# Absolute values on ScalarE, small copies set free, and a new order, in a fused mLSTM and ELU feed-forward kernel

## The chip, the cores and the metric

The kernel runs on one core of a Trainium2 chip. The core has a matrix engine (TensorE, PE in the profile), three engines for elementwise work (VectorE or DVE, ScalarE or ACT, GpSimd or POOL) and SyncE (SP), which here only issues DMAs. Each engine takes its instructions in order, and they wait for one another through semaphores. The metric is the device time of one execution in microseconds (us).

## The reference

Two stages stand one behind the other. The first is an mLSTM recurrence over 768 positions for 4 batches and 8 heads of width 40:

```
m_new  = max(f_gate[t] + m, i_gate[t])
f_stab = exp(f_gate[t] + m - m_new);  i_stab = exp(i_gate[t] - m_new)
C = f_stab * C + i_stab * outer(v[t], k[t])
n = f_stab * n + i_stab * k[t]
denom = max(abs(n . q[t]), 1)
y[t]  = sigmoid(o_gate[t]) * (C q[t]) / denom
```

The second is a feed-forward network on the 3072 x 320 result, with 2048 hidden columns: `elu(x @ w_in) @ w_out`. All of it is float32.

## The kernel before

**Tiles.** The recurrence is computed in chunks of 128 positions: 6 chunks times 4 batches are 24 tiles, n = 4 c + b. For a chunk, `gate_chunk(c)` works on the gates of all 32 heads at once: a copy of the running maximum `m0` into the first column of `m` (L427), a scan for the maxima (L428), the decays (L433, L434) and the copy of the last maximum back to `m0` (L435), all on VectorE. For a tile, `attention(n)` makes the products k.q (L555), scales the values by the input gates and appends the gates as a 41st column for the denominators (`va`, L563 and L564), builds the decay weights by a scan (L595, on rows that for the first two chunks are spread by small matmuls, L581), multiplies (L609), and sums the outputs in PSUM (L631, from chunk 1 on L623 too). The state C is carried by L644 and the lines behind it. Then come the denominators (L673, L676, L679), the scaling and the result (L683, L687), its transposition by TensorE (L704) and a split into a high and a low part, `xh` and `xl` (L707, L710).

**Weights.** 18 pieces of `w_in` and `w_out`, called c0 to c17, are loaded as float64 words and turned to high and low float32 parts by `conversion(i)`: two operations on ScalarE (L324, L329), three on VectorE (L333, L338, L343), an addition on GpSimd (L348), and the split by ScalarE and, as a rule, VectorE (L354, L358). c0, c1, c2 belong to the first layer for the first four hidden blocks; c3 and c4 to the second layer for hidden blocks 0, 1 and 2, 3; c5 and c6 (with the second half of c2) to the first layer of hidden blocks 4 to 7; c7 and c8 to the second layer of 4, 5 and 6, 7; c9 to c17 to the rest. Pieces of `w_out` have 640 columns, those of `w_in` 512. Three `wide` buffers hold loaded pieces.

**Feed-forward.** Tiles go through the network in blocks of 2, 3, 3, 3, 3, 3, 3, 2 and 2. A step is one hidden block of 128 for one block of tiles: eight products of layer 1 (L746) into a PSUM tile `h` of which there are two, the ELU (L754, L757, L759), its high and low part (L762, L764), and three products for each tile in layer 2 (L773). The first three blocks of tiles are taken through hidden blocks 0 to 7 first, then through 8 to 15 one after the other. The PSUM buffers `h` are also those of the spread matmuls L581.

**What sets the order.** Every operation is registered by `op` with the engines that may take it, with an estimated time for each, and with what it reads and writes. `Plan.run` then makes a list schedule in estimated time: whenever an engine is free it starts the ready operation of the lowest rank that finds its buffers, on the engine that would end it first, and so each engine's queue is fixed when the program is built. An operation with `"port"` is kept off VectorE while an operation on GpSimd, or another such one, runs in the plan. The string `FIRST` ranks the first tiles (t) and conversions (c). The ranks of the others follow from how many steps ahead of their first use they are wanted: LEAD and SPACE for tiles, LEAD_C for conversions. FFN steps rank behind all that they need.

Of the kernel before, what the change touches and what calls it, by code (L numbers as in the profile page):

```python
# [14 lines left out]
AF = mybir.ActivationFunctionType  # L15
ALU = mybir.AluOpType
# [4 lines left out]
P = 128  # L21
# [162 lines left out]
def tile_mlstm_then_elu_ffn(  # L184
# [11 lines left out]
    nc = tc.nc  # L196
# [3 lines left out]
    H, S = 2 * HH, NC * L  # L200
# [12 lines left out]
    TMAX = max(BLOCKS)  # L213
    WMAX = max(512, W2N * DM)

    FIRST = "t0c0c1c4t1c2c6c5c8t2c3c7c9"

    LEAD, SPACE, LEAD_C = 4, 3, 2

    R2 = 64 + D  # L220
    ROWS = [slice(64 * two, 64 * two + D) for two in range(2)]
# [9 lines left out]
    def copy(e, o, i):  # L231
        nc.scalar.copy(o, i) if e == "ACT" else eng[e].tensor_copy(o, i)
# [28 lines left out]
    def T(name, i, *shape, dt=F32, part=""):  # L261

        if (name, i, part) not in tiles:
            tiles[name, i, part] = pools[name].tile(list(shape), dt, name=name + part)
        return tiles[name, i, part]
# [148 lines left out]
    def gate_chunk(c):  # L414
        def f():
            return T("gates", c, BH, L, part="f")

        def i():
            return T("gates", c, BH, L, part="i")

        def m():
            return T("gates", c, BH, L + 1, part="m")

        KF, KI, KM, FI = ("gates", c, "f"), ("gates", c, "i"), ("gates", c, "m"), ("first", 0)

        def top(e):
            nc.vector.tensor_copy(m()[:, 0:1], m0)  # L427
            nc.vector.tensor_tensor_scan(m()[:, 1:], f(), i(), m0, op0=ALU.add, op1=ALU.max)  # L428

        op({"port": 1, "DVE": 0.6}, top, (KF, KI, ("m0", 0)), (KM,))  # L430

        def log_decay(e):
            nc.vector.tensor_add(f(), f(), m()[:, 0:L])  # L433
            nc.vector.tensor_sub(f(), f(), m()[:, 1:])  # L434
            nc.vector.tensor_copy(m0, m()[:, L : L + 1])  # L435

        op({"port": 1, "DVE": 0.66}, log_decay, (KM,), (KF, ("m0", 0)))
        op({"port": 1, "POOL": 0.4, "DVE": 0.27}, lambda e: eng[e].tensor_sub(i(), i(), m()[:, 1:]), (KM,), (KI,))
        op({"ACT": 0.3}, lambda e: nc.scalar.activation(f(), f(), AF.Exp), (), (KF,))
        op({"ACT": 0.3}, lambda e: nc.scalar.activation(i(), i(), AF.Exp), (), (KI,))  # L440

        def starts(e):

            nc.vector.tensor_copy(first[:, 0:1], f()[:, 0:1])
            nc.vector.memset(f()[:, 0:1], 0.0)

        def parts(e):
            starts(e)
            rest = [f()] + [pools["rest"].tile([BH, L], F32, name=f"rest{j}") for j in range(2)]
            for j in range(3):  # L450
                part = fgs[j * BH : (j + 1) * BH, c * L : (c + 1) * L]
                nc.vector.tensor_copy(part, rest[j])
                if j < 2:
                    nc.vector.tensor_sub(rest[j + 1], rest[j], part)

        if c < SPREAD_BY_PE:
            op({"port": 1, "DVE": 1.5}, parts, (KF,), (FI, KF, ("fgs", c)))
        else:
            op({"port": 1, "DVE": 0.2}, starts, (KF,), (FI, KF))
            op({"SP": 0.06}, lambda e: nc.sync.dma_start(f_d[c], f()), (KF,), (("f_d", c),),  # L460
               nbytes=BH * L * 4)

        def turned():
            return T("ps_a", ("iT", c), P, BH)

        KT = ("ps_a", ("iT", c))
        op({"PE": 0.35}, lambda e: nc.tensor.transpose(turned(), i(), ident[:BH, :BH]),
           (KI, ("ident", 0)), (KT,))
        op({"DVE": 0.19, "ACT": 0.25}, lambda e: copy(e, iT[:, c, :], turned()),
           (KT,), (("iT", c),))  # L470
        if c > 0:

            op({"port": 1, "DVE": 0.42},
               lambda e: nc.vector.tensor_tensor_scan(
                   i(), f(), first, 0.0, op0=ALU.mult, op1=ALU.add),
               (KF, FI), (KI,))
            op({"SP": 0.06}, lambda e: nc.sync.dma_start(b_d[c], i()), (KI,), (("b_d", c),),
               nbytes=BH * L * 4)
# [34 lines left out]
    def attention(n):  # L513
# [11 lines left out]
        def v3():  # L525
            t3 = T("vko", n, P, 3, H, D)
            return [t3[:, j] for j in range(3)]

        def va():
            return T("va", n, P, H, E)  # L530
# [8 lines left out]
        def dec():  # L539
            return T("dec", n, R2, HH, 1)  # L540

        def den(part=""):
            return T("den", n, P, H, 1, part=part)

        def ps(which, *shape):
            return T("ps_a", (n, which), *shape)
# [12 lines left out]

        op({"PE": 1.25}, products, KQ + (("w", n, "room"),), tuple(("ps_a", (n, two)) for two in range(2)))  # L560

        def values(e):
            eng[e].tensor_mul(va()[:, :, 0:D], v3()[0], ib.to_broadcast([P, H, D]))  # L563
            eng[e].tensor_copy(va()[:, :, D:E], ib)  # L564

        op({"port": 1, "POOL": 0.95, "DVE": 0.6}, values, (KV, ("iT", c)), (("va", n),))

        for fn, kw in ((AF.Exp, dict(scale=-1.0)), (AF.Ln, dict(bias=1.0)), (AF.Exp, dict(scale=-1.0))):
            op(act(H * D),
# [46 lines left out]
        def outputs(e):  # L616
# [19 lines left out]

        KY, KU = ("ps_a", (n, "y")), ("ps_a", (n, "u"))
        op({"PE": 1.6 if c else 0.9}, outputs,
           (("w", n, 0), ("w", n, 1), ("va", n)) + (KB + (("C", b),) if c else ()), (KY, ("given", n)))
        if c < NC - 1:  # L640

            def update(e):
                for h in range(H):
                    nc.tensor.matmul(  # L644
                        ps("u", P, HH, E)[ROWS[h % 2], h // 2, :], v3()[1][:, h, :], va()[:, h, :],
                        start=True, stop=True, skip_group_check=True,
                    )

            op({"PE": 0.5}, update, (KK, ("va", n), ("given", n)), (KU,))
            if c > 0:  # L650

                def shrink(e):
                    for two, rows in enumerate(ROWS):
                        cv = C[b][rows, :, two, :]
                        eng[e].tensor_mul(cv, cv, dec()[rows].to_broadcast([D, HH, E]))  # L655

                op({"port": 1, "POOL": 1.06, "DVE": 0.6}, shrink, (("dec", n),), (("C", b),))

            def gather(e):
                for two, rows in enumerate(ROWS):  # L660
                    cv = C[b][rows, :, two, :]
                    u = ps("u", P, HH, E)[rows]
                    if c == 0:
                        copy(e, cv, u)
                    else:
                        nc.vector.tensor_add(cv, cv, u)

            op({"ACT": 0.58, "DVE": 0.5} if c == 0 else {"DVE": 0.64}, gather, (KU,), (("C", b),))


        def denominators(e):
            y = ps("y", P, H, E)
            nc.vector.tensor_scalar(  # L673
                den("neg"), y[:, :, D:E], -1.0, 1.0, op0=ALU.mult, op1=ALU.max
            )
            nc.vector.scalar_tensor_tensor(  # L676
                out=den(), in0=y[:, :, D:E], scalar=1.0, in1=den("neg"), op0=ALU.max, op1=ALU.max
            )
            nc.vector.reciprocal(den(), den())  # L679

        op({"DVE": 0.5}, denominators, (KY,), (("den", n),))
        op(two_in(H * D),
           lambda e: eng[e].tensor_mul(v3()[2], v3()[2], den().to_broadcast([P, H, D])),  # L683
           (("den", n),), (KS,))
# [218 lines left out]
```

## Time and profile before

| | before |
|---|---|
| device time, median of 3 runs | 495.1 us (493.95 to 495.77) |
| the profiled execution's own time | 494.69 us |
| its span, first to last instruction | 492.6 us |
| mean granted TensorE clock | 0.991 of full speed |
| TensorE matmuls busy | 456.1 us |
| VectorE busy | 362.2 us |
| ScalarE busy | 288.4 us |
| GpSimd busy | 117.6 us |

All times inside the trace count from the start of the span. The shares of busy time are averages over a start, in which the weights are converted and the first tiles made, and a long stage of feed-forward steps; they have to be read by stretch.

### The profile page before, as it was taken

How to read it: one execution, taken by the hardware profiler on the slowest of the kernel's cores; microseconds unless marked ns; L12 is line 12 of the kernel's file. 1: busy time of each engine (PE TensorE's matmuls, PEld its weight loads, DVE VectorE, ACT ScalarE, POOL GpSimd, SP SyncE). 2: the span in 40 equal slices, each digit the busy share in tenths (PEclk: the TensorE clock that was granted, in tenths of full speed). 3: DMA queues.
4: the chain of work that ended last, by engine and by line, in shares of the span. 5: the costliest groups of instructions: out<-in, count | busy, mean ns of one | idle time of the engine just before them, and what ended most of it. 6: DMA issues, size and time to landing. Idle time of an engine off the chain costs nothing.

```text
span 492.6 us, 12520 instructions
## 1 busy us (share of the span) xinstructions
PE 456.1 (93%) x5006; PEld 432.6 (88%) x5006; DVE 362.2 (74%) x752; ACT 288.4 (59%) x681; POOL 117.6 (24%) x151
## 2 busy tenths in 40 slices
PE   2535889999999999999999999999999999999997
PEld 2334878999999999999989999999999999999996
DVE  8989898998787987965896478873678365546543
ACT  3555945779876564646456464475447544654664
POOL 2444484244231253121220101430012031000000
PEclk9999979999999999999999999999999999999999
DMA  7665544433325353421441034540333030100000
GB/s 266 176 208 166 167 136 138 134 110 127 106 82 154 100 164 110 154 84 42 133 145 43 28 110 127 153 124 1 111 111 109 1 97 1 43 1 1 28 1 27
DMA packets 39001, 49.51 MB, mean 101 GB/s; under 512 B 3072, under 2 KB 31648, under 8 KB 38944
## 3 DMA queue, kind: packets, MB, share of 16 engines
q1 hardware_dynamic: 38944, 48.72, 31.9%
q8 instruction: 39, 0.64, 0.5%
q14 instruction: 18, 0.15, 0.1%
HBM read 43.32 MB, written 5.39 MB: 99 GB/s over the span
## 4 chain that ended last, share of the span: by engine, by line
PE 86%; DVE 11%; ACT 2%; issue 1%; DVEq 0%; ACTq 0%
PE h L746 36%; PE acc L773 34%; PE ps_a L555 5%; PE ps_a L631 3%; PE ps_a L623 3%; DVE w L595 2%; PE ps_a L644 1%; PE ps_a L704 1%; DVE narrow L343 1%; DVE w L358 1%; DVE narrow L333 1%; DVE e L759 1%; DVE narrow L338 1%; PE h L581 1%; DVE w L609 1%
## 5 line engine op out<-in xcount | busy, mean ns | idle before, releaser
L746 PE MATMUL h<-xh,w 128*128 128x384 f32 (+1 forms) x720 | 179.6, 325 | 3.6 <-DVE w L595 2.2
L773 PE MATMUL acc<-w,gh 128*128 128x320 f32 x768 | 175.4, 315 | 1.5 <-DVE w L358 1.5
L773 PEld LDWEIGHTS acc<-w,gh 128*128 128x128 f32 x768 | 128.3, 189 | 3.9 <-DVE w L358 1.7
L746 PEld LDWEIGHTS h<-xh,w 128*128 128x128 f32 x720 | 126.1, 189 | 6.4 <-DVE w L595 2.6
L759 DVE SCALAR_TENSOR_TENSOR e<-e,h 128x384 f32<-128x384 f32 (+1 forms) x144 | 72.7, 505 | 72.6 <-ACT e L757 71.9
L754 ACT ACTIVATE e<-h 128x384 f32<-128x384 f32 (+1 forms) x144 | 65.4, 454 | 101.8 <-PE h L746 96.0
L773 PE MATMUL acc<-w,gl 128*128 128x320 f32 x384 | 119.3, 311 | 0.0
L746 PE MATMUL h<-xl,w 128*128 128x384 f32 (+1 forms) x432 | 113.0, 320 | 0.0
L762 ACT CAST gh<-e 128x384 fp32r<-128x384 f32 (+1 forms) x144 | 67.8, 472 | 34.9 <-DVE e L759 34.8
L764 DVE TENSOR_TENSOR gl<-e,gh 128x384 fp32r<-128x384 f32 (+1 forms) x118 | 64.1, 544 | 27.0 <-ACT gh L762 23.9
L746 PEld LDWEIGHTS h<-xl,w 128*128 128x128 f32 x432 | 77.1, 189 | 0.0
L773 PEld LDWEIGHTS acc<-w,gl 128*128 128x128 f32 x384 | 72.5, 189 | 0.8 <-DVE gl L764 0.6
L757 ACT ACTIVATE e<-e 128x384 f32<-128x384 f32 (+1 forms) x144 | 70.5, 490 | 3.8
L595 DVE TENSOR_TENSOR_SCAN w<-w,ident 128x512 f32<-128x512 f32 x32 | 40.0, 1249 | 5.6 <-DMA w<-f_d 5.4
L764 POOL TENSOR_TENSOR gl<-e,gh 128x384 fp32r<-128x384 f32 (+1 forms) x26 | 25.4, 978 | 63.2 <-ACT gh L762 59.0
L348 POOL TENSOR_TENSOR narrow<-narrow,wide 128x512 int32<-128x512 int32 (+1 forms) x18 | 27.4, 1523 | 41.9 <-DVE narrow L343 24.5
L570 ACT ACTIVATE vko<-vko 128x320 f32<-128x320 f32 x72 | 33.6, 467 | 2.7 <-DMA vko<-in_vko 1.9
L555 PE MATMUL ps_a<-qk 40*128 40x128 f32 x384 | 32.4, 316 | 0.0
L609 DVE TENSOR_TENSOR w<-ps_a,w 128x512 f32<-128x512 f32 x48 | 31.1, 679 | 1.3 <-PE ps_a L555 0.8
L555 PEld LDWEIGHTS ps_a<-qk 40*128 40x128 f32 x384 | 27.4, 216 | 4.4 <-issue 3.7
L655 POOL TENSOR_TENSOR C<-C,dec 40x164 f32<-40x164 f32 x28 | 16.1, 576 | 60.8 <-PE ps_a L623 59.8
L563 POOL TENSOR_TENSOR va<-vko,iT 128x320 f32<-128x320 f32 x15 | 14.1, 938 | 65.6 <-issue 33.4
(87 smaller groups left out, 419.8 us busy)
## 6 DMA issues: line engine op xcount, KB each, us to landing
vko<-in_vko SPq DMA_DIRECT2D x24, 480.0 KB
w<-f_d SPq DMA_DIRECT2D x32, 256.0 KB
qk<-in_qk SPq DMA_DIRECT2D x48, 160.0 KB
wide<-in_w_out SPq DMA_DIRECT2D x8, 640.0 KB
wide<-in_w_in SPq DMA_DIRECT2D x8, 512.0 KB
out<-os SPq DMA_DIRECT2D x24, 160.0 KB
bb<-b_d SPq DMA_DIRECT2D x40, 80.0 KB
sum<-os SPq DMA_DIRECT2D x8, 160.0 KB
```

What stands on the lines that cost most here:

```text
L348: lambda e: nc.gpsimd.tensor_add(narrow(), narrow(), words()[0]),
L555: nc.tensor.matmul(ps(two, P, HH, L)[:, j, :], kt[rows, j, :], qt[rows, j, :], start=True, stop=True,)
L570: lambda e, fn=fn, kw=kw: nc.scalar.activation(v3()[2], v3()[2], fn, **kw), (), (KS,))
L595: nc.vector.tensor_tensor_scan(a, f, ident4.rearrange("p h t -> p (h t)"), 0.0, op0=ALU.mult, op1=ALU.add)
L609: lambda e, half=half: nc.vector.tensor_mul(w(half), ps(half, P, HH, L), w(half)),
L746: nc.tensor.matmul(h(), a[g][:, fs], m, start=(i == 0), stop=(i == len(prods) - 1))
L754: op(act(N), lambda e, h=h, ff=ff: nc.scalar.activation(ff("e"), h(), AF.Relu, scale=-1.0), (KHP,), (KE,))
L757: lambda e, ff=ff: nc.scalar.activation(ff("e"), ff("e"), AF.Exp, scale=-1.0), (), (KE,))
L759: lambda e, h=h, ff=ff: nc.vector.scalar_tensor_tensor(out=ff("e"), in0=ff("e"), scalar=-1.0, in1=h(), op0=ALU.add, op1=ALU.max),
L762: op(act(N), lambda e, ff=ff: nc.scalar.copy(ff("gh", F32R), ff("e")), (KE,), (KG,))
L764: lambda e, ff=ff: eng[e].tensor_sub(ff("gl", F32R), ff("e"), ff("gh", F32R).bitcast(F32)),
L773: nc.tensor.matmul(acc(a), x[:, sl], bw[g][:, j, :], start=(f == f0 and i == 0), stop=(f == f1 - 1 and i == 2),)
```

## The change

The absolute value of the denominators is taken by ScalarE, straight from PSUM, and VectorE only clamps and inverts it in SBUF. The copies into `m`, back to `m0`, and of the gates into the 41st column of `va` become operations of their own that ScalarE may take (for `va` GpSimd too); the keys of `va` are split for that. `FIRST` and LEAD_C are changed, and the whole program is planned anew.

```
-    FIRST = "t0c0c1c4t1c2c6c5c8t2c3c7c9"
-    LEAD, SPACE, LEAD_C = 4, 3, 2
+    FIRST = "t0c0c4t1c8c5c1c2t2c6c3c7c9"
+    LEAD, SPACE, LEAD_C = 4, 3, 0
...
-        def top(e):
-            nc.vector.tensor_copy(m()[:, 0:1], m0)
-            nc.vector.tensor_tensor_scan(m()[:, 1:], f(), i(), m0, op0=ALU.add, op1=ALU.max)
-        op({"port": 1, "DVE": 0.6}, top, (KF, KI, ("m0", 0)), (KM,))
+        op({"ACT": 0.2, "DVE": 0.13}, lambda e: copy(e, m()[:, 0:1], m0), (("m0", 0),), (KM,))
+        op({"port": 1, "DVE": 0.48},
+           lambda e: nc.vector.tensor_tensor_scan(
+               m()[:, 1:], f(), i(), m0, op0=ALU.add, op1=ALU.max),
+           (KF, KI, ("m0", 0)), (KM,))
+        op({"ACT": 0.2, "DVE": 0.13}, lambda e: copy(e, m0, m()[:, L : L + 1]), (KM,), (("m0", 0),))
...
-            nc.vector.tensor_copy(m0, m()[:, L : L + 1])
-        op({"port": 1, "DVE": 0.66}, log_decay, (KM,), (KF, ("m0", 0)))
+        op({"port": 1, "DVE": 0.54}, log_decay, (KM,), (KF,))
...
-        def values(e):
-            eng[e].tensor_mul(va()[:, :, 0:D], v3()[0], ib.to_broadcast([P, H, D]))
-            eng[e].tensor_copy(va()[:, :, D:E], ib)
-        op({"port": 1, "POOL": 0.95, "DVE": 0.6}, values, (KV, ("iT", c)), (("va", n),))
+        op({"port": 1, "POOL": 0.75, "DVE": 0.49},
+           lambda e: eng[e].tensor_mul(va()[:, :, 0:D], v3()[0], ib.to_broadcast([P, H, D])),
+           (KV, ("iT", c)), (("va", n, 0),))
+        op({"port": 1, "ACT": 0.2, "POOL": 0.2, "DVE": 0.17},
+           lambda e: copy(e, va()[:, :, D:E], ib), (("iT", c),), (("va", n, 1),))
...
+        op({"ACT": 0.22},
+           lambda e: nc.scalar.activation(den(), ps("y", P, H, E)[:, :, D:E], AF.Abs),
+           (KY,), (("den", n),))
         def denominators(e):
-            y = ps("y", P, H, E)
-            nc.vector.tensor_scalar(
-                den("neg"), y[:, :, D:E], -1.0, 1.0, op0=ALU.mult, op1=ALU.max
-            )
-            nc.vector.scalar_tensor_tensor(
-                out=den(), in0=y[:, :, D:E], scalar=1.0, in1=den("neg"), op0=ALU.max, op1=ALU.max
-            )
+            nc.vector.tensor_scalar_max(den(), den(), 1.0)
             nc.vector.reciprocal(den(), den())
-        op({"DVE": 0.5}, denominators, (KY,), (("den", n),))
+        op({"port": 1, "DVE": 0.3}, denominators, (), (("den", n),))
```

## Rows read from the trace of the kernel before

**Rows 1.** The page's first part: busy time, share and instructions of each engine.

```profile
PE 456.1 (93%) x5006; PEld 432.6 (88%) x5006; DVE 362.2 (74%) x752; ACT 288.4 (59%) x681; POOL 117.6 (24%) x151
```

**Rows 2.** Stretches of time: length, busy us by engine, granted clock, DMA.

```profile
core 0: us, PE busy (x) PEld busy (x) DVE busy (x) ACT busy (x) POOL busy (x), PEclk, DMA share, GB/s
0.00:47.00 47.00, 18.35 (x327) 15.08 (x327) 42.77 (x86) 24.00 (x50) 19.18 (x29) 1.00 0.65 209
47.00:75.00 28.00, 24.52 (x310) 21.70 (x311) 24.97 (x56) 19.02 (x50) 15.89 (x21) 0.88 0.49 150
75.00:492.60 417.60, 413.23 (x4371) 395.83 (x4370) 294.50 (x611) 245.38 (x582) 82.54 (x103) 1.00 0.28 85
```

**Rows 3.** TensorE's waits: who, for whom, total us, times, longest.

```profile
PE h L581 <- DVE w L595: 15.9, 5, 8.0
PE acc L773 <- DVE w L358: 1.5, 1, 1.5
```

**Rows 4.** Timeline of TensorE: start us, us, line, operation, idle before and releaser.

```profile
41.82 0.85 PE L704 MATMUL ps_a<-ident,xf 128*128 128x128 f32 x3
...
47.05 0.58 PE L746 MATMUL h<-xh,w 128*128 128x256 f32 x1 [1.72 <-DVE w L595]
...
55.05 0.56 PE L773 MATMUL acc<-w,gh 128*128 128x320 f32 x2 [1.50 <-DVE w L358]
...
81.36 0.34 PE L746 MATMUL h<-xh,w 128*128 128x384 f32 x1
```

**Rows 5.** Timeline of VectorE: tile 1's result; ends of c2, c5, c8, c17.

```profile
31.88 0.49 DVE L687 TENSOR_TENSOR xf<-ps_a,vko 128x320 f32<-128x320 f32 x1
...
34.49 2.37 DVE L358 TENSOR_TENSOR w<-narrow,w 64x512 fp32r<-64x512 f32 x2
...
42.46 0.68 DVE L358 TENSOR_TENSOR w<-narrow,w 128x512 fp32r<-128x512 f32 x1
...
48.21 0.82 DVE L358 TENSOR_TENSOR w<-narrow,w 128x640 fp32r<-128x640 f32 x1
...
147.74 0.79 DVE L358 TENSOR_TENSOR w<-narrow,w 128x640 fp32r<-128x640 f32 x1
```

**Rows 6.** Stretches around the low granted clock (columns as in rows 2).

```profile
65.00:70.00 5.00, 3.69 (x30) 3.28 (x32) 4.90 (x9) 2.07 (x7) 4.85 (x6) 0.78 0.48 119
70.00:80.00 10.00, 10.00 (x218) 9.01 (x217) 8.13 (x18) 4.42 (x12) 7.02 (x10) 0.77 0.45 152
```

**Rows 7.** Stretch 0 to 75 us of L673, L564 and L427 alone.

```profile
core 0: us, DVE busy (x), PEclk, DMA share, GB/s
0.00:75.00 75.00, 0.82 (x5) 0.95 0.59 187
...
core 0: us, DVE busy (x) POOL busy (x), PEclk, DMA share, GB/s
0.00:75.00 75.00, 0.17 (x1) 1.52 (x5) 0.95 0.59 187
...
0.00:75.00 75.00, 0.28 (x2) 0.95 0.59 187
```

**Rows 8.** Groups by line and shape: count, busy us, mean ns, idle before.

```profile
L676 DVE SCALAR_TENSOR_TENSOR den<-ps_a,denneg 128x8 f32<-128x8 f32 x24 | 4.0, 166 | 0.8
L679 DVE RECIPROCAL den<-den 128x8 f32<-128x8 f32 x24 | 4.9, 203 | 0.8
L232 ACT COPY iT<-ps_a 128x32 f32<-128x32 f32 x4 | 0.7, 177 | 0.1
L595 DVE TENSOR_TENSOR_SCAN w<-h,ident 128x512 f32<-128x512 f32 x16 | 19.0, 1207 | 0.5 <-PE h L581 0.4
L609 DVE TENSOR_TENSOR w<-ps_a,w 128x512 f32<-128x512 f32 x48 | 31.1, 679 | 1.3 <-PE ps_a L555 0.8 <-ACT wl L232 0.2
```

**Rows 9.** Timeline of GpSimd and VectorE: L333 beside L348, and alone.

```profile
20.09 1.28 POOL L348 TENSOR_TENSOR narrow<-narrow,wide 128x512 int32<-128x512 int32 x1 [3.23 <-ACT vko L570]
20.35 1.38 DVE L333 TENSOR_SCALAR narrow<-narrow 128x640 f32<-128x640 f32 x1
...
48.95 0.48 DVE L333 TENSOR_SCALAR narrow<-narrow 128x640 f32<-128x640 f32 x1
```

**Rows 10.** The chain that ended last, in order of time: last steps of block 0.

```profile
146.57 1.92 PE h L746 x16
...
151.66 1.76 PE acc L773 x12
```

More of the change, by code (lines that the diff above doesn't have):

```diff
@@ L540, in dec, with den @@
             return T("dec", n, R2, HH, 1)
-        def den(part=""):
-            return T("den", n, P, H, 1, part=part)
+        def den():
+            return T("den", n, P, H, 1)
         def ps(which, *shape):
@@ L638, in attention @@
         op({"PE": 1.6 if c else 0.9}, outputs,
-           (("w", n, 0), ("w", n, 1), ("va", n)) + (KB + (("C", b),) if c else ()), (KY, ("given", n)))
+           (("w", n, 0), ("w", n, 1), ("va", n, 0), ("va", n, 1)) + (KB + (("C", b),) if c else ()), (KY, ("given", n)))
         if c < NC - 1:
@@ L647, in update @@
                     )
-            op({"PE": 0.5}, update, (KK, ("va", n), ("given", n)), (KU,))
+            op({"PE": 0.5}, update, (KK, ("va", n, 0), ("va", n, 1), ("given", n)), (KU,))
             if c > 0:
```

## The prediction

> **What bounds the kernel now.** I read the busy times first, then the share of each engine in stretches of time, then TensorE's own waits, then the timeline around the places that these point at. TensorE is busy for 456.1 of 492.6 us, VectorE for 362.2 [rows 1]. The stretches show where the 36.5 us without a matmul lie: 28.65 of them before 47 us, 3.5 between 47 and 75, and 4.4 in all the 417.6 after that [rows 2]. From about 81 us on this is a TensorE kernel, and nothing that VectorE, ScalarE or GpSimd does there can be seen unless it becomes later than TensorE's queue. Up to about 75 us VectorE is the bound: it is busy for 67.7 of 75 us [rows 2]. TensorE's waits say the same: 15.9 us of them are attention's spread matmuls (L581) that wait for a VectorE scan to free the PSUM buffer that they share with the FFN [rows 3]. So one number stands for the whole start: the first product of 384 columns, where the block of three tiles begins, at 81.36 us [rows 4]. Behind it lies a fixed amount of TensorE work; what moves that start moves the end.
>
> Three readings inside the start matter. First, tile 1's result was finished by VectorE at 32.37 us [rows 5], yet its transposition ran at 41.82 [rows 4], since TensorE takes its queue in order and two spreads that waited for scans stood before it. Secondly, the first product of layer 1 ran at 47.05, and layer 2 began at 55.05, released by the last VectorE operation of the w_out conversion c3 [rows 3, 4]. Thirdly, TensorE was busy for only 3.69 of the 5 us from 65 and then ran at a lower granted clock: 0.78 of full speed on average from 65 to 70 us and 0.77 from 70 to 80 [rows 6], with the lower of the two levels (1.2 GHz) in between. At 2.4 GHz this stretch would have cost 0.22 x 5 + 0.23 x 10 = 3.4 us less.
>
> **The change, part by part.** Terms are against the profiled execution's own time, 494.69 us: span 492.6 and 2.09 around it. That execution is 0.4 below the median of the three (495.1) and inside their spread.
>
> (a) Less on VectorE before 75 us. Five tiles run their denominators there [rows 7]. Before, each takes a maximum (0.16), a combined maximum (0.17) and a reciprocal (0.20) [rows 7, 8], 0.53 us; after, one maximum, taken at 0.16 like the nearest one-input row, and the reciprocal: 0.17 less, five times, 0.83. The `va` copy ran once on VectorE in that time (0.17; the other five were on GpSimd already), and the two gate chunks' copies into `m` took 0.28 [rows 7]; the copies back to `m0` (L435) are as many and as small, another 0.28. If all go to ScalarE that is 1.56 us. Nothing of ScalarE's share is on the path: its nearest row, a copy of 128x32 from PSUM, takes 0.18 us [rows 8], and it is idle for 32 of the first 75 us [rows 2]. Without that cover an absolute value would cost its 0.18 plus whatever conversion work queues behind it on ScalarE while it waits for the outputs' matmuls; VectorE's first denominator operation waits at that place today, so the wait moves with it and is not new. Queued behind it on ScalarE are the next conversion's L324, L329 and L354 and the L570 of the next tile, and VectorE waits for those; but VectorE has other work of that kind at hand all through the start. The copy into `m` adds one wait on the path of chunk 0, where VectorE's scan comes right behind it: between 0 (VectorE keeps the copy) and 0.18 for ScalarE's copy less the 0.14 that VectorE saves; taken as 0.
>
> What stands against it: the new maximum reads and writes SBUF, where the old one read PSUM. The trace shows what an SBUF-only operation with a constant can meet: L333 at 128x640 took 1.38 us while GpSimd's addition ran from 20.09 to 21.37, and 0.48 when it ran at 48.95 beside an idle GpSimd [rows 9]; the reciprocal, also in SBUF and with one input, shows no stretch in its mean of 203 ns over all 24 [rows 8], so both ends are possible for a new form. If it stretches, GpSimd being busy for 35.1 of 75 us (47%) [rows 2], a maximum meets one of its operations about every second time and waits for half of it, 0.64: 0.47 x 0.64 x 5 = 1.5 us, which would eat the gain. Bounds: 0 and 1.5. I take 0.7, since the planner now keeps this operation out of GpSimd's planned time but real times differ from planned ones. The Trainium skill, "SBUF — State Buffer", section "Who interferes with whom", has the rule for the second end: VectorE and GpSimd share one pair of ports as an exclusive lock, and a copy or an operation with a constant that uses both ports fully blocks until the other engine's instruction is over. By that rule alone the term would be -1.5 and (a) nil; L333's end, 0.36 us after GpSimd's, agrees with it. (a) = -1.56 + 0.7 = -0.85 us.
>
> (b) The order of the first conversions. Before c3, the same work stands in both orders: tiles 0 to 2 and c0, c1, c2, c4, c5, c6, c8. So the last VectorE operation ahead of layer 2 should end at about the same time, and I take nothing. Within that, tile 1 comes ahead of c1, and c1 and c2, which the first product needs, come behind c8 and c5. Tile 1's product is thus ready earlier (it stood waiting for 9.5 us anyway) and c2 later: c2 ended at 36.86 before [rows 5] and had 10.2 us in hand until 47.05. It was the fourth conversion loaded and is now the sixth; three `wide` buffers hold the loads, so it follows the second and third buffer to come free. Bounds: the two scans (1.21 each) and two products (0.68 each) of tile 3 that ran on VectorE ahead of c3's end although they rank later [rows 8] could fall behind it, -3.8 us; or c2 could become the bound, +3.5 (below).
>
> (c) The pause near 65 us. VectorE with less to do should reach the scan and the FFN step that TensorE waited for some tenths of a us earlier. I expect that the pause becomes short enough for the clock to stay up. TensorE then gets 3.4 us back, but only as much is worth having as VectorE can follow: in the low-clock stretch from 70 to 80 us VectorE stood idle for 1.87 us [rows 6]. So -1.9, with the bounds 0 and -3.4.
>
> (d) Later conversions ranked two steps later (LEAD_C). The last one ended at 148.53 [rows 5], and the two steps of layer 2 that use it began at 151.66 [rows 10]: 3.1 us in hand. Two steps of two tiles are 1.92 + 1.76 = 3.7 us of TensorE [rows 10], so it could lose 0.6 us, and only if the planner let it wait for all of its new rank. Taken as 0.
>
> (e) Past 148 us every removed or moved operation lies beside TensorE work: 0. The gate copies gain a wait between engines per chunk, off the path there.
>
> Sum: -0.85 - 1.9 = -2.75, so 491.9 us.
>
> **Rivals.**
> *A much shorter start.* Tile 3's scans fall behind c3, so layer 2 starts 3.8 us earlier, all of the 1.56 arrives, and the pause vanishes: 494.69 - 3.8 - 1.56 - 1.9 = 487.4. For it: tile 1's transposition need not wait behind spreads, as TensorE reaches them sooner. Against it: the spreads are placed by a planner that fills idle TensorE time with whatever fits, which was what let tile 3 in.
> *The relief is eaten.* The new maximum meets GpSimd as L333 did, and the pause and the low clock stay: 494.7. For it: 47% GpSimd share; against it: the order is planned around that.
> *Slower: c2 becomes the bound.* Place: the first product of layer 1. As a late load c2 could end where the seventh conversion ended before, c8 at 49.03, plus 1.55 for its second half (2.37 against 0.82) [rows 5]: 50.6. The first product is then 3.5 us later than 47.05, layer 2 behind it as well, and the end: 498.2. It decides from the point where c2's last operation ends later than 47 us. For it: two w_out conversions, the longer kind (640 columns against 512), hold two of the three buffers ahead of it. Against it: the sixth load before, c5, was done by 43.14 us [rows 5], inside the time in hand.
>
> **How the numbers follow.** A measurement of this kernel can tell about 0.5%, 2.5 us, from no change: faster ends at 492.6, slower begins at 497.6. Forecast 0.44 (from 489.7 to 494.7, a little more than half of it under 492.6: 0.26 faster, 0.18 same); the shorter start 0.24, all faster; the eaten relief 0.12, all same; c2 late 0.20, all slower. Together 0.50, 0.30 and 0.20. The range reaches from 487 to 498.5: it takes in both bounds of (a), (b) and (c) less the corners where several fall together.
>
> **What would show it.** (a): denominators of two VectorE operations and one of ScalarE, none of VectorE's maxima beyond 0.3 us where GpSimd is idle, VectorE's sum before 75 us smaller. (b): tile 1's transposition before 35 us, c2's last operation after 38 but before 47, layer 2 near 54. (c): granted clock 1.00 from 65 to 80 us, and the first product of 384 columns at about 78.6 instead of 81.36. (d): no TensorE wait between 130 and 155 us. The prediction is wrong if that first 384-column product moves and the end doesn't move with it, or if TensorE gains new pauses behind 81 us.

## The result

The changed kernel takes 490.24 us (median of 7 runs, 490.01 to 491.43) against 495.03 (7 runs, 492.77 to 496.36): ratio 0.991, 95% interval 0.989 to 0.993. It is faster by 0.9%. The profiled execution has an own time of 490.24 and a span of 488.4, 4.2 less than the span of before. The forecast was 491.9.

The page's first part, of after [against rows 1]:

```profile
PE 459.8 (94%) x5006; PEld 434.2 (89%) x5006; DVE 368.7 (75%) x745; ACT 298.3 (61%) x746; POOL 80.4 (16%) x93
```

TensorE was busy for longer than before (459.8 against 456.1) in a shorter span: what fell is its idle time, 488.4 - 459.8 = 28.6 us against 36.5. GpSimd lost a third of its work (80.4 against 117.6), ScalarE gained 9.9 us.

Stretches of after, columns as in [rows 2]; the last three answer to [rows 6]:

```profile
0.00:47.00 47.00, 26.93 (x362) 22.04 (x362) 43.54 (x85) 29.46 (x72) 18.44 (x26) 1.00 0.72 229
47.00:75.00 28.00, 24.89 (x291) 22.49 (x294) 24.50 (x52) 18.35 (x51) 8.97 (x11) 0.82 0.37 105
75.00:488.40 413.40, 407.97 (x4375) 389.71 (x4362) 300.71 (x610) 250.47 (x623) 53.00 (x56) 1.00 0.28 87
...
60.00:65.00 5.00, 4.09 (x25) 3.57 (x26) 4.66 (x8) 2.73 (x10) 3.29 (x4) 0.60 0.42 132
65.00:70.00 5.00, 4.56 (x28) 4.07 (x25) 3.95 (x6) 1.75 (x4) 1.01 (x2) 0.50 0.36 106
70.00:75.00 5.00, 5.00 (x92) 4.65 (x95) 4.21 (x10) 2.49 (x8) 0.91 (x2) 0.88 0.22 63
```

TensorE gets ahead in the first 47 us: 362 products instead of 327, and 20.1 us without one instead of 28.65. From 60 to 75 us the granted clock is low, 0.60, 0.50 and 0.88; before it was low only from 65 us on (0.78 from 65 to 70 and 0.77 from 70 to 80 [rows 6]).

TensorE's waits of after, as in [rows 3]:

```profile
PE h L581 <- DVE w L595: 11.5, 6, 3.2
```

The wait of 8.0 us is gone, the longest is 3.2, and the sum for L581 fell from 15.9 to 11.5. Layer 2's wait of 1.5 us for c3 is gone as well: its first product, at 52.42 below, has no idle time before it. A wait for a later conversion, c7, stands at 66.53.

Timeline of TensorE in after, columns as in [rows 4]:

```profile
27.45 0.90 PE L702 MATMUL ps_a<-ident,xf 128*128 128x128 f32 x3
...
41.41 0.56 PE L744 MATMUL h<-xh,w 128*128 128x256 f32 x1
...
52.42 0.46 PE L771 MATMUL acc<-w,gh 128*128 128x320 f32 x2
...
60.91 0.54 PE L581 MATMUL h<-fgs,sel 96*128 96x128 bf16 x4 [2.04 <-DVE w L595]
...
64.01 2.08 PE L555 MATMUL ps_a<-qk 40*128 40x128 f32 x16
...
66.53 0.90 PE L771 MATMUL acc<-w,gh 128*128 128x320 f32 x2 [0.44 <-DVE w L358]
...
82.61 0.45 PE L744 MATMUL h<-xh,w 128*128 128x384 f32 x1
```

Tile 1's transposition came 14.4 us earlier than in [rows 4], the first product of layer 1 5.6 and layer 2 2.6. Then comes a pause of 2.04 us before 60.91, the lower clock behind it (the 16 products of L555 took 2.08), and the first product of 384 columns 1.25 us later than before.

How can the end come 4.2 us earlier, if that product comes later? A start of one operation says only how far that operation got. I counted all products that had started by a point, each kind at a fixed time taken from its groups at full clock in these traces (0.118 us for 256 columns in layer 1, 0.176 for 384, 0.147 in layer 2, 0.0725 in L555, and so on). The sum is an estimate of the TensorE work done, in us; the last column is the span:

```
by (us)                       47    60    75    85   110   span
before                      11.9  21.2  31.2  41.9  66.5  492.6
after                       15.4  25.1  34.8  43.7  68.8  488.4
order alone (e4)            14.4  21.9  31.2  41.6  66.2  491.9
old denominators (e11)      14.7  24.9  33.3  42.4  66.8  492.0
copies on VectorE (e12)     14.7  24.3  32.3  41.5  66.4  490.8
one pause filled (e9)       15.3  25.1  33.3  42.5  67.5  491.8
pauses filled, 58-67 (e10)  15.3  25.1  35.9  45.0  69.8  488.1
```

After is 3.5 us of work ahead by 47 us and still 2.3 ahead by 110. (With the small products at the distance from one start to the next, 0.068 us in L555, every sum is 3 to 7 us lower, but a row's distance from the row of before changes by at most 0.5.) The first 384-column product is later because more of the attention work and of the two-tile steps ran before it.

### The profile page after: what moved, and what is told of

It is laid out like the page before. It is cut to its first block, busy times and chain, and to the rows that moved or that the text cites. A ratio compares the mean times of both kernels' runs of the same rounds, so it can differ in the third digit from the quotient of the medians.

```text
span 488.4 us, 12469 instructions
## 1 busy us (share of the span) xinstructions
PE 459.8 (94%) x5006; PEld 434.2 (89%) x5006; DVE 368.7 (75%) x745; ACT 298.3 (61%) x746; POOL 80.4 (16%) x93
## 4 chain that ended last, share of the span: by engine, by line
PE 83%; DVE 9%; ACT 3%; DMA 3%; issue 1%; POOL 0%; SPq 0%; DVEq 0%; ACTq 0%
PE h L744 35%; PE acc L771 33%; PE ps_a L555 5%; PE ps_a L631 4%; PE ps_a L623 3%; DVE w L595 2%; PE ps_a L644 1%; PE ps_a L702 1%; DMA bb<-b_d 1%; DVE narrow L343 1%; PE h L581 1%; DMA w<-f_d 1%; DMA wide<-in_w_in 1%; DVE w L358 1%; DVE e L757 1%
## 5 line engine op out<-in xcount | busy, mean ns | idle before, releaser
L744 PE MATMUL h<-xh,w 128*128 128x384 f32 (+1 forms) x720 | 184.7, 329 | 2.9 <-DVE w L595 1.6
L744 PEld LDWEIGHTS h<-xh,w 128*128 128x128 f32 x720 | 128.2, 193 | 6.0 <-DVE e L757 2.2
L762 DVE TENSOR_TENSOR gl<-e,gh 128x384 fp32r<-128x384 f32 (+1 forms) x132 | 70.3, 537 | 31.8 <-ACT gh L760 30.8
L744 PEld LDWEIGHTS h<-xl,w 128*128 128x128 f32 x432 | 78.5, 193 | 0.0
L595 DVE TENSOR_TENSOR_SCAN w<-w,ident 128x512 f32<-128x512 f32 x32 | 38.9, 1217 | 6.7 <-DMA w<-f_d 6.6
L348 POOL TENSOR_TENSOR narrow<-narrow,wide 128x512 int32<-128x512 int32 (+1 forms) x18 | 27.1, 1504 | 52.3 <-DVE narrow L343 21.5
L555 PE MATMUL ps_a<-qk 40*128 40x128 f32 x384 | 34.0, 317 | 0.0
L555 PEld LDWEIGHTS ps_a<-qk 40*128 40x128 f32 x384 | 28.4, 216 | 5.3 <-issue 4.0
L609 DVE TENSOR_TENSOR w<-ps_a,w 128x512 f32<-128x512 f32 x48 | 31.5, 682 | 2.0 <-PE ps_a L555 1.8
L563 POOL TENSOR_TENSOR va<-vko,iT 128x320 f32<-128x320 f32 x18 | 14.4, 808 | 72.3 <-PE ps_a L644 27.4
L631 PE MATMUL ps_a<-va,w 128*32 128x41 f32 x1536 | 21.7, 213 | 0.2
L631 PEld LDWEIGHTS ps_a<-va,w 128*32 128x32 f32 x1536 | 18.5, 118 | 3.2 <-issue 0.6
```

What stands on the lines that cost most here:

```text
L555: nc.tensor.matmul(ps(two, P, HH, L)[:, j, :], kt[rows, j, :], qt[rows, j, :], start=True, stop=True,)
L595: nc.vector.tensor_tensor_scan(a, f, ident4.rearrange("p h t -> p (h t)"), 0.0, op0=ALU.mult, op1=ALU.add)
L609: lambda e, half=half: nc.vector.tensor_mul(w(half), ps(half, P, HH, L), w(half)),
L631: nc.tensor.matmul(y[r, h, :], w()[:, i, r], va()[:, h, :], start=not opened, stop=(i == H - 1), skip_group_check=True,)
L744: nc.tensor.matmul(h(), a[g][:, fs], m, start=(i == 0), stop=(i == len(prods) - 1))
L762: lambda e, ff=ff: eng[e].tensor_sub(ff("gl", F32R), ff("e"), ff("gh", F32R).bitcast(F32)),
```

## Where VectorE's time went

In the kernel before, the last VectorE operation of c3 released layer 2. It ended at 55.00 us before and at 51.23 after, where layer 2 (52.42) no longer waits for it. VectorE's busy time up to there, first before, then after (length, busy and count):

```profile
0.00:55.00 55.00, 24.84 (x370) 20.92 (x370) 49.77 (x98) 30.81 (x66) 22.39 (x32) 1.00 0.65 209
```

```profile
0.00:51.23 51.23, 30.53 (x448) 25.19 (x450) 47.48 (x92) 32.72 (x80) 20.26 (x27) 1.00 0.70 223
```

Of the 3.77 us, 2.29 are less busy time (third pair, 49.77 to 47.48) and 1.48 less idle (5.23 to 3.75). Groups of VectorE's operations in these stretches show which. Before (count, then busy us and mean ns, then idle time ahead and its releaser):

```profile
L358 DVE TENSOR_TENSOR w<-narrow,w 128x640 fp32r<-128x640 f32 x3 | 2.5, 830 | 0.9 <-ACT w L354 0.8
...
L333 DVE TENSOR_SCALAR narrow<-narrow 128x640 f32<-128x640 f32 x3 | 2.4, 784 | 0.0
L358 DVE TENSOR_TENSOR w<-narrow,w 64x512 fp32r<-64x512 f32 x2 | 2.3, 1171 | 0.1
...
L338 DVE TENSOR_SCALAR narrow<-narrow 128x640 int32<-128x640 int32 x3 | 2.0, 666 | 0.1
...
L683 DVE TENSOR_TENSOR vko<-vko,den 128x320 f32<-128x320 f32 x3 | 1.8, 600 | 0.0
...
L673 DVE TENSOR_SCALAR denneg<-ps_a 128x8 f32<-128x8 f32 x3 | 0.5, 161 | 1.0 <-PE ps_a L631 1.0
```

After:

```profile
L358 DVE TENSOR_TENSOR w<-narrow,w 128x640 fp32r<-128x640 f32 x3 | 2.5, 827 | 0.2 <-ACT w L354 0.2
...
L681 DVE TENSOR_TENSOR vko<-vko,den 128x320 f32<-128x320 f32 x3 | 1.5, 497 | 0.0
L338 DVE TENSOR_SCALAR narrow<-narrow 128x640 int32<-128x640 int32 x3 | 1.5, 491 | 0.1
...
L333 DVE TENSOR_SCALAR narrow<-narrow 128x640 f32<-128x640 f32 x3 | 1.4, 476 | 0.0
L358 DVE TENSOR_TENSOR w<-narrow,w 64x512 fp32r<-64x512 f32 x2 | 1.4, 686 | 0.1
...
L676 DVE TENSOR_SCALAR den<-den 128x8 f32<-128x8 f32 x3 | 0.5, 165 | 0.0
```

These are the same operations in the same number (but for the denominators), and four groups lost 2.7 us (2.4 + 2.3 + 2.0 + 1.8 against 1.5 + 1.5 + 1.4 + 1.4); the other shape of L333 gained 0.4. They were stretched beside GpSimd, and are not now. The clearest case is the pair of c2, which took 2.37 us from 34.49 on [rows 5], beside this operation of GpSimd:

```profile
34.69 1.62 POOL L348 TENSOR_TENSOR narrow<-narrow,wide 128x512 int32<-128x512 int32 x1 [1.70 <-DVE narrow L343]
```

In after the pair takes 1.40, at 40.86, with GpSimd idle. The small operations themselves count for less: 1.75 us by their rows left VectorE there (copies into C, which the new plan gave to ScalarE, 0.60; one of the denominators 0.5; the others 0.65), and 1.9 us of other work that ran later before came in (1.3 of FFN steps and a scaling, 0.6 of a product L609 that started at 54.92 before). So nearly all of the 2.29 us is stretching that is gone: 2.7 - 0.4 + 1.75 - 1.9 = 2.15, and rows overlap by some tenths. Of the idle time, 1.0 us was the old denominators' wait for the outputs' products (L673), which now falls to ScalarE's Abs, and 0.6 c3's wait for ScalarE's L354.

## The experiments

**Single parts alone.** e1: the kernel before with the new FIRST. e2: the kernel before with LEAD_C = 0. e4: with both. e3: the changed kernel with the old FIRST and LEAD_C, so the new operations alone.

```diff
# e1
-    FIRST = "t0c0c1c4t1c2c6c5c8t2c3c7c9"
+    FIRST = "t0c0c4t1c8c5c1c2t2c6c3c7c9"
# e2
-    LEAD, SPACE, LEAD_C = 4, 3, 2
+    LEAD, SPACE, LEAD_C = 4, 3, 0
# e4: both of these, on the kernel before
# e3: both of these undone, on the changed kernel
```

> The kernel before with the new string FIRST alone. Theory A (the order of the first conversions makes the gain: tile 1 comes ahead of c1, so TensorE gets tile 1's outputs and transposition some 14 us earlier and begins layer 1 near 41 instead of 47 us): 490.5 to 491.5 us, tile 1's transposition before 30 us. Theory B (the forecast's term: less work for VectorE makes the gain, the order nothing): 494 to 496 us. Theory C (any new plan moves the start by a few us by chance, the parts don't add up): anywhere from 488 to 499, and not with the sign of A.

> The kernel before with LEAD_C = 0 alone. The forecast's step (d) and theory A: no change, 494.5 to 495.5 us, no TensorE wait from 130 to 155 us. The rival to (d), that conversions ranked later reach TensorE late: 495.5 to 497 us with a wait for L358 or L354 in that stretch. Theory C: a shift of 2 us or more in either direction that arises before 85 us.

> The kernel after with the old FIRST and LEAD_C, so the edits of operations alone (absolute value on ScalarE, free small copies). Theory B (relief of VectorE before 75 us): 492 to 493.5 us. Theory A: 494 to 495.5 us, tile 1's transposition still after 38 us. Theory C: off from both by 2 us or more.

> The kernel before with both order edits, FIRST and LEAD_C, and no edit of operations. Theory A: 490.5 to 491.5 us, like FIRST alone. Theory B: 494 to 496 us. Theory C: differs from FIRST alone by 2 us or more though LEAD_C alone does nothing.

Measured against 495.31 (35 runs): e1 493.84, ratio 0.9986 [0.9967, 1.0004]; e2 494.40, 0.9986 [0.9968, 1.0003]; e3 495.11, 1.0000 [0.9983, 1.0018]; e4 493.05, 0.9974 [0.9955, 0.9994]. The operations alone give nothing, the order alone 0.26%, together they give 0.92%. So the two need each other, as far as these kernels tell it: each of them was planned anew, and a plan alone can move more than that (e7 and e11 below). e3's time is the one that theory A expected, but its tile 1 was transposed at 32.05 us, not after 38 (41.82 in before): that this comes early brought nothing there. The times of e1 and e4 lie between what A and B expected. Why the order alone isn't enough, TensorE's waits of e4 show:

```profile
PE h L581 <- DVE w L595: 8.8, 5, 3.5
...
PE h L746 <- DVE e L759: 4.9, 2, 3.4
PE ps_a L631 <- DVE w L609: 3.5, 2, 2.6
```

The long spread wait is gone here too, but TensorE now waits for VectorE elsewhere: for a two-tile FFN step (3.4) and a masked score product (2.6). It is 2.5 us ahead by 47 us and level with before by 75 (the table above). And e4 has a collision of its own. First GpSimd, then VectorE, in its timeline:

```profile
27.12 1.56 POOL L348 TENSOR_TENSOR narrow<-narrow,wide 128x640 int32<-128x640 int32 x1 [3.21 <-DMA gatesf<-in_f_gate]
...
27.53 1.49 DVE L683 TENSOR_TENSOR vko<-vko,den 128x320 f32<-128x320 f32 x1
```

The multiplication vko·den took 1.49 us here and ended 0.34 after GpSimd's addition, as L333 did in [rows 9]. The same operation in before:

```profile
31.36 0.48 DVE L683 TENSOR_TENSOR vko<-vko,den 128x320 f32<-128x320 f32 x1
```

**Parts taken back, planned anew.** e5: the changed kernel with LEAD_C = 2. e7: with the old denominators. e8: with the old copies.

```diff
# e5
-    LEAD, SPACE, LEAD_C = 4, 3, 0
+    LEAD, SPACE, LEAD_C = 4, 3, 2
# e7
-        op({"ACT": 0.22},
-           lambda e: nc.scalar.activation(den(), ps("y", P, H, E)[:, :, D:E], AF.Abs),
-           (KY,), (("den", n),))
...
-            nc.vector.tensor_scalar_max(den(), den(), 1.0)
+            y = ps("y", P, H, E)
+            nc.vector.tensor_scalar(
+                den("neg"), y[:, :, D:E], -1.0, 1.0, op0=ALU.mult, op1=ALU.max
+            )
+            nc.vector.scalar_tensor_tensor(
+                out=den(), in0=y[:, :, D:E], scalar=1.0, in1=den("neg"), op0=ALU.max, op1=ALU.max
+            )
...
-        op({"port": 1, "DVE": 0.3}, denominators, (), (("den", n),))
+        op({"DVE": 0.5}, denominators, (KY,), (("den", n),))
# e8: top(), log_decay() and values() as in the kernel before
```

> The kernel after with LEAD_C back at 2. Theory D (the edits of operations and the new FIRST only work together, LEAD_C is nothing): 489.5 to 491 us. Theory E (a lucky plan that needs all three): 492 to 495 us.

> The kernel after with the denominators as before, three operations on VectorE from PSUM. If the relief of VectorE by the absolute value carries its part of the gain (0.83 us by the forecast's term): 490.8 to 492 us. If the denominators carry nothing: 489.7 to 490.7 us. If only the whole plan works: 492.5 us or more.

> The kernel after with the small copies as before (into m and back to m0 on VectorE inside their neighbours, the gates' column of va on the engine of the product before it). If the forecast's 0.73 us for them holds: 490.8 to 491.5 us. If freeing these copies is what lets TensorE start earlier together with the order: 492.5 us or more. If they carry nothing: 489.7 to 490.7.

Measured against 495.00 (20 runs): e5 490.75, 0.9927 [0.9907, 0.9948]; e7 497.33, 1.0057 [1.0039, 1.0076]; e8 492.89, 0.9961 [0.9943, 0.9979]. LEAD_C is worth nothing that can be measured. Without the Abs the kernel is slower than before. But the planner wrote another order for e7 and e8, so these two mix the operation's price and the plan's. That called for the next pair.

**Parts taken back, the plan kept.** The planner is left with the costs of the changed kernel, so that it writes the same order, and only the function that an operation issues is exchanged. e11: the Abs operation issues nothing, and the VectorE operation issues the old three. e12: the gate copies and the copy into `va` run on VectorE.

```diff
# e11
-           lambda e: nc.scalar.activation(den(), ps("y", P, H, E)[:, :, D:E], AF.Abs),
+           lambda e: None,
...
-            nc.vector.tensor_scalar_max(den(), den(), 1.0)
+            # the two operations of e7
# e12
-        op({"ACT": 0.2, "DVE": 0.13}, lambda e: copy(e, m()[:, 0:1], m0), (("m0", 0),), (KM,))
+        op({"ACT": 0.2, "DVE": 0.13}, lambda e: copy("DVE", m()[:, 0:1], m0), (("m0", 0),), (KM,))
...
-        op({"ACT": 0.2, "DVE": 0.13}, lambda e: copy(e, m0, m()[:, L : L + 1]), (KM,), (("m0", 0),))
+        op({"ACT": 0.2, "DVE": 0.13}, lambda e: copy("DVE", m0, m()[:, L : L + 1]), (KM,), (("m0", 0),))
...
-           lambda e: copy(e, va()[:, :, D:E], ib), (("iT", c),), (("va", n, 1),))
+           lambda e: copy("DVE", va()[:, :, D:E], ib), (("iT", c),), (("va", n, 1),))
```

> The plan of the kernel after, kept to the instruction, but the denominators by the three old VectorE operations at the place of the two new ones, and nothing on ScalarE. If the price of the operations is what counts (0.17 to 0.2 us for each of five tiles): 490.8 to 491.8 us. If the 497.3 of the kernel with the old denominators and a plan of its own came from the operations: 496 us or more. If it came from the plan, as I now think: not above 492.

> The plan of the kernel after, kept to the instruction, but the copies into m, back to m0 and of the gates' column all on VectorE, at their places in the plan. Price of the operations alone (five va copies at 0.17 and three gate copies at 0.14 before 75 us): 490.8 to 491.8 us. If freeing the copies from VectorE is the key: 492.5 us or more.

Measured against 495.32 (20 runs): e11 494.06, 0.9980 [0.9966, 0.9995]; e12 492.54, 0.9947 [0.9930, 0.9964]. So in one and the same order the denominators are worth 494.06 - 490.24 = 3.8 us and the copies 2.3 (3.6 and 1.9 by the ratios to before), where the expectation for e11 was at most 491.8 by the price of one operation of some 0.2 us for each tile, and not above 492 in any case: that was wrong. The two prices sum to 6.1 us, more than the whole gain of 4.8: they aren't shares of it, and no run takes out both in this order. e11's timeline shows where the price grows. GpSimd and VectorE:

```profile
16.85 0.73 POOL L563 TENSOR_TENSOR va<-vko,iT 128x320 f32<-128x320 f32 x1
17.00 0.93 DVE L687 TENSOR_TENSOR vko<-vko,den 128x320 f32<-128x320 f32 x1
...
40.25 0.72 POOL L563 TENSOR_TENSOR va<-vko,iT 128x320 f32<-128x320 f32 x1
40.30 1.02 DVE L687 TENSOR_TENSOR vko<-vko,den 128x320 f32<-128x320 f32 x1
...
51.78 0.83 DVE L358 TENSOR_TENSOR w<-narrow,w 128x640 fp32r<-128x640 f32 x1 [0.19 <-ACT w L354]
```

The same places in after:

```profile
16.80 0.47 DVE L681 TENSOR_TENSOR vko<-vko,den 128x320 f32<-128x320 f32 x1
16.85 1.00 POOL L563 TENSOR_TENSOR va<-vko,iT 128x320 f32<-128x320 f32 x1
...
39.36 0.54 DVE L681 TENSOR_TENSOR vko<-vko,den 128x320 f32<-128x320 f32 x1
39.51 0.96 POOL L563 TENSOR_TENSOR va<-vko,iT 128x320 f32<-128x320 f32 x1
...
40.86 1.40 DVE L358 TENSOR_TENSOR w<-narrow,w 64x512 fp32r<-64x512 f32 x2
...
50.40 0.83 DVE L358 TENSOR_TENSOR w<-narrow,w 128x640 fp32r<-128x640 f32 x1 [0.16 <-ACT w L354]
```

In these four meetings whichever of the two starts second pays. In after VectorE's multiplication starts 0.05 and 0.15 us ahead of GpSimd's and takes 0.47 and 0.54, and GpSimd's is stretched to about 1.0. In e11 VectorE comes 0.15 and 0.05 us behind, GpSimd's takes 0.72, and VectorE's 0.93 and 1.02. The one extra operation is 0.20 us, three times before c3; the two collisions lost are 0.46 and 0.48: 1.54 in all, and c3 indeed ends 1.38 later. This part is shown. From there to 3.8 us it is counted, not traced from link to link: e11 is 1.5 us of TensorE work behind after by 75 us and 2.0 by 110, and its first 384-column product starts at 84.05 instead of 82.61. And e7, with its own order, is another 3.3 us slower than e11 with the order of after: a plan alone is worth as much as a part of the change.

In e12 the copies have a price that their own length doesn't show either. Its VectorE groups up to 75 us:

```profile
L232 DVE COPY va<-iT 128x8 f32<-128x8 f32 x6 | 2.1, 358 | 0.0
...
L232 DVE COPY gatesm<-m 32x1 f32<-32x1 f32 x3 | 0.4, 138 | 0.1
L232 DVE COPY m<-gatesm 32x1 f32<-32x1 f32 x2 | 0.3, 132 | 0.0
```

The copy into `va` takes 0.358 on average, where the one of before took 0.17 [rows 7]. That mean comes from one of the six, beside GpSimd's L348 (1.56 us from 20.28 on); the others take 0.15 to 0.17:

```profile
20.54 1.34 DVE L232 COPY va<-iT 128x8 f32<-128x8 f32 x1
```

So a copy that is placed without regard to GpSimd cost eight times its length here. Together with the four gate copies that ScalarE has in after, these are 2.1 + 2 x 0.138 + 2 x 0.132 = 2.6 us of VectorE, and 2.3 us at the end.

**The pause and the clock.** e9, e10 and e13 are the changed kernel in the same plan with products of zeros added into `acc` where TensorE pauses; they don't change the sums. The zeros themselves are written by GpSimd at the start, and this holds up all that follows:

```profile
4.38 0.46 POOL L408 MEMSET zero<- 128x448 bf16 x1
```

By this the copy into `va` on GpSimd comes at 9.03 in e10 instead of 8.65: the three kernels start with a loss of 0.38 us. e9 adds 13 before the second spread of tile 4. e10 adds 12 there, 4 before the first spread of tile 5 and 11 before the fifth step of layer 2. e13 fills the pauses before 47 us as well.

```diff
+    FILL = {(4, 1): 12, (5, 0): 4}                                            # e9: {(4, 1): 13}
+    FILL_ACC = {4: 11}                                                        # e9: none
+    # e13: FILL = {(2, 0): 4, (2, 1): 3, (3, 0): 14, (3, 1): 9, (4, 1): 12, (5, 0): 4}, 5 before a step of layer 1
+    def fill(count):
+        for _ in range(count):
+            nc.tensor.matmul(T("acc", (0, 0), P, 512)[:, 0:DM], zero[:, 0:P], zero[:, P:],
+                             start=not begun, stop=False, skip_group_check=True)
...
+                fill(FILL.get((n, half), 0))
...
+                fill(FILL_ACC.get(k, 0))
```

> The kernel after, same plan, with 13 products of zeros into an accumulator just ahead of the spread that TensorE waits 2.04 us for at 58.9 us, so that TensorE is busy in this pause. The clock theory (the pause lets the clock fall, which costs 5.1 us of TensorE time from 60 to 75): granted clock near 1.00 from 60 to 75 us, and 486.5 to 488.5 us. The VectorE theory (from 47 to 85 us VectorE sets the pace, so a fast TensorE only waits more): clock near 1.00 but 489.7 to 490.7 us. If the filler does not hold the clock: clock 0.5 to 0.6 there as before and 490 to 491 us.

> The kernel after, same plan, with products of zeros (they add nothing) ahead of three places where TensorE waits between 58 and 68 us: 12 ahead of the second spread of tile 4, 4 ahead of the first of tile 5, 11 ahead of the fifth step of layer 2. Clock theory: granted clock near 1.00 from 55 to 76 us and the end 2 to 5 us earlier than the kernel after, 485.5 to 488.5 us. VectorE theory: the clock holds and the end stays, 489.5 to 491 us, with longer TensorE waits for VectorE in its place. If only the pause that is left lets the clock fall somewhere else by 85 us: 489.5 to 492 us and a low stretch there.

> As the one before, and also products of zeros in the pauses before 47 us (4, 3, 14 and 9 ahead of the spreads of tiles 2 and 3, 5 ahead of the second step of layer 1), so that TensorE is busy from 17 us on. Clock theory: the products of keys and queries fall from 2.08 to about 1.16 us per tile before 47 us, and a further 1 to 2 us is saved. VectorE theory: those products get faster and the end doesn't move by more than 0.7 us against the kernel without these. Slower if the products of zeros are themselves what the spreads wait for.

e9: 491.22 (9 runs, 489.62 to 493.53), ratio 0.9934 [0.9914, 0.9955]. The profiled execution is the longest of them (493.53), and shows why filling one pause isn't enough. Stretches of e9:

```profile
60.00:65.00 5.00, 4.24 (x38) 3.27 (x38) 4.96 (x8) 3.75 (x12) 3.54 (x4) 1.00 0.35 103
65.00:70.00 5.00, 3.39 (x25) 3.00 (x22) 3.92 (x7) 1.75 (x4) 1.04 (x2) 0.65 0.39 123
```

The clock stays at 1.00 past the filled pause; TensorE, now faster, meets the next pause (1.61 us before the layer-2 product at 67.23, for the last operation of c7), and the clock falls behind that one. So e10 fills this one too. Stretches of e10:

```profile
60.00:65.00 5.00, 4.77 (x42) 3.49 (x41) 4.96 (x8) 3.83 (x12) 3.46 (x4) 1.00 0.34 90
65.00:70.00 5.00, 4.91 (x45) 3.84 (x42) 4.95 (x8) 1.74 (x4) 1.12 (x2) 1.00 0.39 126
70.00:75.00 5.00, 5.00 (x117) 4.59 (x117) 4.83 (x12) 2.90 (x10) 0.92 (x2) 1.00 0.38 121
```

Now the clock is 1.00 in all of these 15 us, and e10 takes 490.16 (0.9905 [0.9884, 0.9926]) where after takes 490.24: no difference, with intervals of about 0.2% to either side. With the 0.38 us of the start, what the clock gives back here is 0.5 us, not to be told from nothing. VectorE is busy for 14.7 of these 15 us, against 12.8 in after: TensorE at full clock has caught up with VectorE. By count TensorE is about 1 us ahead at 75 and 110 us; such a gain is too small to be told from none in the end. e13 takes 489.28 (6 runs, 488.32 to 491.38; 0.9887 [0.9864, 0.9910]); its interval lies below before by at least 0.9%, but overlaps that of after. In it the products of L555 near 25 and 38 us run at full clock (14 of the 16 in 1.16 us, where after takes 2.83 for 16), those before 20 us don't (2.08). It is the lowest median of all, and not shown to be better than after; its two theories, 1 to 2 us more against at most 0.7, are not told apart by the 0.9 between e13 and e10.

## Why the prediction was right, and where it was not

The sign was right and the size inside the range: 2.75 us forecast, 4.45 measured between the two profiled executions. That it came so near is luck: the largest term, (c), is not what happened, and the two others are mis-sized.

**(c), forecast -1.9: this step failed.** "I expect that the pause becomes short enough for the clock to stay up": the pause stayed, only earlier (2.04 us before 60.91), and the low clock lasted longer. What it took from 47 to 75 us, as 28 us times the part of the clock not granted, is 28 x 0.18 = 5.0 us against 28 x 0.12 = 3.4 [rows 2]. And e10 shows that holding the clock there moves the end by 0.08 us, 0.5 with the loss at its start, which is no more than the measurement can tell: nothing shows the 1.9. The prediction had the likely reason in hand (VectorE idle for only 1.87 us of the low-clock stretch) and used it only to halve the price.

**(b), forecast 0: mis-sized.** "Before c3, the same work stands in both orders" is right by count, but the same work did not take the same time: c3 ended 3.77 us earlier, nearly as much as the whole gain. The bound of -3.8 came true, though not by the mechanism named for it: tile 3's two scans still ran ahead of c3 (at 38.27 and 43.83). What changed is how operations of VectorE meet those of GpSimd (2.7 us in four groups), and the idle time. Tile 1's transposition (27.45, "before 35"), c2's end (42.26, "between 38 and 47") and layer 2 (52.42, "near 54") came as written.

That the earlier end of c3 is the gain is not shown. The same operation in e1, then in e8:

```profile
52.09 0.97 DVE L358 TENSOR_TENSOR w<-narrow,w 128x640 fp32r<-128x640 f32 x1
...
53.32 0.82 DVE L358 TENSOR_TENSOR w<-narrow,w 128x640 fp32r<-128x640 f32 x1 [0.64 <-ACT w L354]
```

In e1 c3 ends at 53.06, 1.94 earlier than before, and the profiled execution takes 494.96 us; in e8 it ends at 54.14, 0.86 earlier, and the execution takes 491.37. So c3 tells where after got ahead of before, and not what a plan is worth at the end.

**(a), forecast -0.85: mis-sized.** Of the operations that the prediction listed (1.56 us up to 75 us), 0.8 us left VectorE before c3: 0.49 of the denominators, 0.17 for `va` and 0.14 for `m0`. The other 0.95 of the 1.75 us are copies that it did not count. The 0.7 set against it was not there; the new maximum up to 75 us (shortest, median and longest, in ns):

```profile
L676 DVE TENSOR_SCALAR den<-den x4: 164/165/171, 15.4 to 51.3; 128x8 f32<-128x8 f32 x4
```

None of the four is stretched, and none meets GpSimd: they start at 15.39, 24.82, 37.95 and 51.30, and GpSimd, idle at each of these times, begins its next operation at 15.61, 26.14, 38.26 and 52.60. Later one of the 24 took 0.655. So the planned order kept them clear, as the prediction hoped for in part; that such an operation can't be stretched is not shown. And the worth of an operation removed was taken as its own length; e11 measures 3.8 us for a part whose own length before 75 us is 0.8 (one operation of 0.20 for each of four tiles), and e12 2.3 us for one of 1.6 (six copies of 0.17 and the four gate copies, 0.54). The Trainium skill, "SBUF — State Buffer", section "Who interferes with whom", from which the 1.5 was weighed, says that operations of the two engines can shut each other out, and that the one issued first keeps the shared ports while the other waits. The rows agree with it, but up to 75 us for other operations than the new maximum: vko·den at 0.93 to 1.49 instead of 0.48, the c2 pair at 2.37 instead of 1.40.

**(d) and (e), forecast 0: nothing speaks against them.** e2 (0.9986, not to be told from 1) and e5 (490.75 against 490.24) agree, and no TensorE wait stands between 120 and 160 us in after. Past 85 us TensorE's waits don't grow.

**The rivals.** c2 late: fell, with 42.26 for its end. Relief eaten: fell. Shorter start: its result (c3 earlier by 3.8) was right, its cause wrong, and its 487.4 too far, since the pause didn't vanish.

**The one number.** "The first product of 384 columns" was to stand for the whole start. It came 1.25 us later while the end came 4.2 us earlier. It fails since the planner decides how much other work goes ahead of it; the work done by 110 us (2.3 us ahead) is the better measure, if not a full one: e12 is level with before at 110 and its span is 1.8 us shorter.

**What stays open.** Of the 4.2 us about 2 come after 110 us, in small amounts that no row gathers. Executions of one kernel differ by more than that (before: 492.77 to 496.36), and one profile of each can't settle it. How e11's 1.4 us at c3 become 3.8 at the end is in the same way only partly accounted for.

## What to carry to other kernels

When one engine is the bound and shares its memory's access with another, price a small operation that leaves it not by its own length alone but by which operations then meet: a shift of 0.2 us decided here which engine waited, and VectorE paid 0.5 for it. To learn what a part of a change is worth in a planned kernel, exchange the operation and keep the plan; a new plan alone moved 3.3 us. And compare progress by the work done at a time, not by when one chosen operation starts.

## What the hardware showed that was not expected

Filling a pause of TensorE moved the fall of the clock to the next pause (e9: 1.00 from 60 to 65 us, 0.65 from 65 to 70), and filling three held 1.00 from 60 to 75 us (e10) without moving the end by more than can be told.

Where VectorE and GpSimd each multiply 128x320 from SBUF, a start 0.05 us earlier or later decided which one is stretched: VectorE 0.47 and GpSimd 1.00 us in after, 1.02 and 0.72 in e11. The prediction had weighed such a meeting only for an operation with a constant.

The clock's record in the start is not to be relied on: for the first 47 us it shows 1.00 in after and 0.69 in e11, though the 16 products of L555 that start at 10.48 take 2.08 us in both, and those near 25 us 2.83 and 2.84, against 1.16 at full clock (53.39 in after). So the mean clock of two executions is no measure of one against the other here.
